# Attention, memory and two MoE layers on one core: scores of the first four tasks in fp32, two heads at once in the halves of the array, mask added by TensorE

## The chip, the cores and the metric

The program runs on one core of a Trainium2 chip. The metric is the device time of a whole execution in microseconds (us). TensorE (PE in the profile) multiplies matrices and writes PSUM, VectorE (DVE) and ScalarE (ACT) do the elementwise work, GpSimd (POOL) the maximum over partitions, and SyncE (SP) issues all DMAs.

## The reference

What is computed, cut to what matters (B=4, H=8, S=576, D=64; 2304 tokens of width 512):

```python
scores = q @ k.T / 8;  scores[causal] = -1e9
a = softmax(scores);   local = a @ v
q_p = phi(q)                            # elu(q) + 1
mem = (q_p @ M_prev) / (q_p @ z_prev + 1e-6)
x = g * mem + (1 - g) * local           # g = sigmoid(beta), per head
x = ((x @ w1) * (x @ w2)) @ w3 @ w_out  # first MoE, widths 512-1024-1024-512
h = x @ w_in                            # second MoE, widths 512-2048-512
out = (h * tanh(softplus(h))) @ w_out2
```

All arrays come as float64 weights or fp32 activations; the result is fp32.

## The kernel before

**Order of work.** The program does not run its operations in the order in which they are written. Each is recorded with an engine, a cost in ns and the buffers it reads and writes (`Recorder.op`, L82), and `schedule` (L111) then plays them through a list scheduler: PE takes its ready operations by their place in the program plus a bias, the other engines by how long a chain hangs on them. What comes out is a fixed order for each engine, and on the chip each engine works through its own order without overtaking. The costs handed to `op` therefore decide the order, and nothing else.

**Attention.** A task is a pair of heads of one batch. For batch 0 a task covers half of the queries (hf 0: queries 0 to 287 against the first 384 keys; hf 1: the rest), so tasks 0 to 3 are the hf 0 tasks of the four pairs, tasks 4 to 7 the hf 1 tasks; later tasks cover all 576 queries. Keys and queries come transposed, 64 rows a head. For a score in about fp32 precision the kernel splits them: `load_qk` (L465) loads keys and queries of one head twice, into rows 0 to 63 and again into 64 to 127 (tile `ld`, two buffers), and `prep` (L473) makes from them the tile `QK`: ACT rounds all of it to fp32r (a CAST), DVE subtracts to get what the rounding lost, in the keys' lower 64 rows and in a second copy of the queries. `SC` (L530) then gets a block of scores from two fp32r matmuls over 128 rows, high and low queries. For an hf 0 task these are three blocks of 288, 160 and 32 queries, all in one PSUM bank (tile `g`, eight banks), hence six matmuls a head. After them DVE adds the causal mask (L560, two instructions a head), ACT copies the first block to SBUF, DVE takes maxima over the blocks, POOL the maximum over partitions (L580). `SE` subtracts it (DVE) and takes the exponential (ACT; tile `e`); `AV` (L604) multiplies by V. `phi` (L488) loads the queries of both heads once more (tile `pl`) and `MEM` (L503) multiplies phi by `M`. In the first twelve tasks AV and MEM are plain fp32 matmuls, which the profile shows as two passes each.

**Weights.** The MoE weights are float64 in HBM. `conv` (L673) loads a 512 KB block and makes fp32 of it with one ACT instruction (L339) and two on DVE (L684, L686). The eight blocks of `w_out` (raw in `wA`, converted in `wB`) and the blocks of `w3` (raw in `wE` or `u`, converted in `wD`) are multiplied on the chip into one matrix (`w3_mm`, L718): 64 fp32 products of 128x512, two passes each. A group of eight products needs all eight blocks of `w_out`. Then the units of the first MoE (`g<-x,...` and `g<-u,wA`) run between the heads, and the second MoE closes the program.

Of the kernel before, what the change touches and what calls it, by code (L numbers as in the profile page):

```python
# [10 lines left out]
BF16 = mybir.dt.bfloat16  # L11
I32 = mybir.dt.int32
AF = mybir.ActivationFunctionType
ALU = mybir.AluOpType
P = 128
# [242 lines left out]
def t_mm(n, m=128):  # L258
    return max(n * 0.433 + 7, m * 0.834)
# [3 lines left out]
def kernel(  # L263
    ctx: ExitStack,
    tc: tile.TileContext,
    qk: bass.AP,
    q: bass.AP,
    v: bass.AP,
    mz: bass.AP,
    beta: bass.AP,  # L270
# [8 lines left out]
    nc = tc.nc  # L279
# [22 lines left out]
    op = rec.op  # L302
# [32 lines left out]
    def act(n, o, i, r, w, psum=False, func=AF.Copy, **kw):  # L335
        if func == AF.Copy:
            op("act", t_act(n, psum), lambda: nc.scalar.copy(out=o(), in_=i()), r, w)  # L337
        else:
            op("act", t_act(n, psum), lambda: nc.scalar.activation(out=o(), in_=i(), func=func, **kw), r, w)  # L339
# [7 lines left out]
        op(eng, t_dve(n) if eng == "dve" else t_pool(n), lambda: e.tensor_tensor(out=o(), in0=a(), in1=b(), op=alu), r, w)  # L347

    mask = const.tile([P, P], BF16, name="mask")
    eps = const.tile([P, 1], F32, name="eps")  # L350
    bt = const.tile([P, NP], F32, name="bt")
    gsc = const.tile([P, NP], F32, name="gsc")
# [11 lines left out]
    nc.vector.memset(eps[0:64], 1e-6)  # L364
    nc.vector.memset(eps[64:128], 1e-9)

    fb, fg, fm_ = Fixed(bt), Fixed(gsc), Fixed(mask)
    fx2 = [Fixed(x2d) for _ in range(2 * B)]
    Vf = buf("V", [P, 2, NJ, 2, DV])
    Vb = buf("V", [P, 2, NJ, 2, DV], F32R)  # L370
# [4 lines left out]
    def triangle():  # L375
        idx, low = tri.tile[:, 0], tri.tile[:, 1]
        nc.vector.memset(mask, 0.0)
        for y in range(1, 4):
            nc.vector.memset(mask[32 * y:32 * y + 32, 0:32 * y], NEG)
        nc.vector.memset(idx[:, 0:1], 0.0)  # L380
        for y in range(5):
            nc.vector.tensor_scalar(out=idx[:, 1 << y:2 << y], in0=idx[:, 0:1 << y], scalar1=float(1 << y), scalar2=None, op0=ALU.add)
        nc.vector.transpose(low, idx)
        nc.vector.tensor_tensor(out=low, in0=idx, in1=low, op=ALU.is_lt)
        for y in range(4):
            r = slice(32 * y, 32 * y + 32)
            nc.vector.tensor_scalar(out=mask[r, r], in0=low[r], scalar1=NEG, scalar2=None, op0=ALU.mult)

    op("dve", 1300, triangle, w=[tri, fm_])


    X = {}
# [32 lines left out]
    class Task:  # L425


        def __init__(self, g, hfs):
            self.g, self.hfs = g, hfs
            self.b, self.p = divmod(g, NP)  # L430
            self.w = HS * len(hfs)
            self.x0 = HS * hfs[0]
            self.nj = NJ if 1 in hfs else 3
            self.banks, self.masks, self.works, self.outs = LAYOUT[hfs]

        def qs(self, q0, q1):
# [25 lines left out]

    def load_qk(T, t):  # L465
        h = 2 * T.p + t
        T.qk = getattr(T, "qk", {})
        d = T.qk[t] = buf("ld", [P, KQ])
        q0 = SK + T.x0
        for y, (a, b) in enumerate({(0,): [(K3, SK + HS)], (1,): [(0, SK), (SK + HS, KQ)], (0, 1): [(0, KQ)]}[T.hfs]):  # L470
            dma(lambda a=a, b=b: d.tile[:, a:b], lambda a=a, b=b: qk[T.b, h, :, a:b], 512 * (b - a), w=[(d, y)])

    def prep(T, t):  # L473
        d = T.qk[t]
        T.Q = getattr(T, "Q", {})
        Q = T.Q[t] = buf("QK", [P, KQ + S], F32R)
        lower = HALF[1]
        parts = {(0,): [(K3, SK + HS)], (1,): [(0, SK), (SK + HS, KQ)], (0, 1): [(0, KQ)]}[T.hfs]
        for y, (a, b) in enumerate(parts):
            act(b - a, lambda a=a, b=b: Q.tile[:, a:b], lambda a=a, b=b: d.tile[:, a:b], [(d, y)], [(Q, ("k", y)), (Q, ("q", y))])  # L480
        k0 = parts[0][0]
        q0, q1 = max(parts[-1][0], SK), parts[-1][1]
        y = len(parts) - 1
        lo(SK - k0, lambda: Q.tile[lower, k0:SK], lambda: d.tile[lower, k0:SK], lambda: Q.tile[lower, k0:SK], [(d, 0), (Q, ("k", 0))], [(Q, ("k", 0))])
        lo(q1 - q0, lambda: Q.tile[:, q0 + S:q1 + S], lambda: d.tile[:, q0:q1], lambda: Q.tile[:, q0:q1], [(d, y), (Q, ("q", y))], [(Q, "l")])
        T.qkeys = [("k", 0), ("q", y), "l"]

    def phi(T):  # L488
        w = T.w
        x1 = buf("pl", [P, S])  # L490
        PH = T.PH = buf("PH", [P, S]) if T.f32 else buf("PH", [P, 2, S], F32R)
        e = PH if T.f32 else buf("t", [P, w])
        xv = lambda: x1.tile[:, 0:w]
        ev = lambda: e.tile[:, 0:w]
        dma(xv, lambda: q[T.b, 2 * T.p:2 * T.p + 2, :, T.x0:T.x0 + w].rearrange("t d s -> (t d) s"), 512 * w, w=[x1])
        act(w, ev, xv, [x1], [e], False, AF.Exp)
        act(w, xv, xv, [x1], [x1], False, AF.Identity, bias=one)
        op("dve", t_dve(w), lambda: nc.vector.scalar_tensor_tensor(out=ev(), in0=ev(), scalar=1.0, in1=xv(), op0=ALU.min, op1=ALU.max), r=[e, x1], w=[e])
        if not T.f32:
            act(w, lambda: PH.tile[:, 0, 0:w], ev, [e], [(PH, 0)])  # L500
            lo(w, lambda: PH.tile[:, 1, 0:w], ev, lambda: PH.tile[:, 0, 0:w], [e, (PH, 0)], [(PH, 1)])
# [26 lines left out]
            act(HS, lambda qs=qs, nz=nz: R.tile[0:nz, qs], lambda pn=pn, nz=nz: pn.tile[0:nz, 0:HS], [pn], [(R, (2, hf))], True)  # L528

    def SC(T, t):  # L530
        Q = T.Q[t]
        T.m = m = buf("t", [P, T.w])
        T.s = []
        mkey = []
        for i, pieces in enumerate(T.banks):
            s = gbuf()
            T.s.append(s)

            def f(s=s, pieces=pieces):
                for j, q0, q1, c in pieces:  # L540
                    o = s.tile[:, c:c + q1 - q0]
                    kc = (j * P + K3) % SK
                    for y in range(2):
                        qc = SK + y * S + q0
                        mm(o, Q.tile[:, kc:kc + P], Q.tile[:, qc:qc + q1 - q0], y == 0, y == 1)

            op("pe", sum(2 * t_mm(q1 - q0) for _, q0, q1, _ in pieces), f, r=[(Q, x) for x in T.qkeys], w=[s])
            for i2, cs, m0, m1 in T.masks:
                if i2 != i:
                    continue  # L550

                def mk(s=s, cs=cs, n=m1 - m0, m0=m0, m1=m1):
                    if len(cs) == 1:
                        o, mv = s.tile[:, cs[0]:cs[0] + n], mask[:, m0:m1]
                    else:
                        d = cs[1] - cs[0]
                        e, x = (d, 1) if 2 * d <= 512 else (d // 2, 2)
                        o = s.tile[:, 0:e * (x + 1)].rearrange("p (a c) -> p a c", c=e)[:, 0:x + 1:x, 0:n]
                        mv = mask[:, m0:m1].unsqueeze(1).to_broadcast([P, 2, n])
                    nc.vector.tensor_tensor(out=o, in0=o, in1=mv, op=ALU.add)  # L560

                op("dve", t_dve((m1 - m0) * len(cs)), mk, r=[s, fm_], w=[s])
            for j, q0, q1, c in pieces:
# [12 lines left out]
            if i + 1 == len(T.banks) or T.banks[i + 1][0][1] != pieces[0][1]:
                x = len(mkey) - 1
                a, b = mkey[x]
                mv = lambda a=a, b=b: m.tile[:, T.qs(a, b)]
                op("pool", 430 + 2.6 * (b - a), lambda mv=mv: nc.gpsimd.partition_all_reduce(mv(), mv(), P, bass_isa.ReduceOp.max), r=[(m, x)], w=[(m, x)])  # L580
# [412 lines left out]
    rec.flush()  # L993


_INS = ['qk', 'q', 'v', 'mz', 'beta', 'moe_w1', 'moe_w2', 'moe_w3', 'moe_w_out', 'moe2_w_in', 'moe2_w_out']
_OUTS = [((2304, 512), 'float32')]


# [47 lines left out]
```

## Time and profile before

| what | value |
|---|---|
| time, median of 3 runs | 965.72 us (965.35 to 968.41) |
| the profiled execution's own time | 965.84 us |
| its span | 964.1 us |
| PE busy / weight loads busy | 945.7 us (98%) / 808.9 us (84%) |
| DVE busy | 725.8 us (75%) |
| ACT busy | 607.0 us (63%) |
| POOL busy | 86.4 us (9%) |
| DMA | 96.62 MB, mean 100 GB/s |

The span runs from the first instruction to the last; 1.7 us of the execution's time lie outside it. Matmuls are pipelined: their recorded ends overlap the next starts, so the spacing of starts tells what one costs, and the busy share of PE says little by itself. PEld is the weight load that precedes each pass.

### The profile page before, as it was taken

Reading aid. Unit: us, or ns where it says so; the run is one execution under the profiler, and the core shown is the slowest. Engines: PE = TensorE matmul, PEld = TensorE weight load, DVE = VectorE, ACT = ScalarE, POOL = GpSimd, SP = SyncE. Lnnn points to the kernel's source line nnn. Section 1 sums busy time; section 2 is a strip of 40 time slices with the busy share of each in tenths; the row PEclk is TensorE's granted clock in tenths of the full one; section 3 lists DMA queues with packets and bytes.
Section 4 is the critical chain, followed back from the end, with each engine's and each line's share of the span. In section 5 each row is a group of like instructions: output and inputs, shape, how many; then the busy total and the mean of one; then the engine's idle time right before and its main releaser. Section 6 shows DMA issues by size and latency. Waiting matters only on the chain.

```text
span 964.1 us, 15222 instructions
## 1 busy us (share of the span) xinstructions
PE 945.7 (98%) x5440; PEld 808.9 (84%) x5440; DVE 725.8 (75%) x1643; ACT 607.0 (63%) x1240; POOL 86.4 (9%) x70
## 2 busy tenths in 40 slices
PE   6999999999999999999999999999999999999998
PEld 3454878778999999999999988888888888998997
DVE  7999999899999989896653987547554756565663
ACT  6677877778797778775433776446444544554653
POOL 1210012322222012120000000000000000000000
PEclk9999999999999999999999999999999999999999
DMA  9689655542433422302641740020002001100000
GB/s 351 215 246 303 201 167 153 156 141 82 142 98 91 151 75 83 107 26 83 203 153 49 228 167 1 1 81 7 1 1 83 1 0 32 46 1 17 34 1 33
DMA packets 48316, 96.62 MB, mean 100 GB/s; under 512 B 11024, under 2 KB 23344, under 8 KB 48240
## 3 DMA queue, kind: packets, MB, share of 16 engines
q1 hardware_dynamic: 48240, 95.64, 31.3%
q8 instruction: 43, 0.70, 0.3%
q14 instruction: 33, 0.27, 0.1%
HBM read 85.85 MB, written 9.77 MB: 99 GB/s over the span
## 4 chain that ended last, share of the span: by engine, by line
PE 67%; DVE 18%; ACT 6%; DMA 4%; issue 3%; SPq 1%; POOL 0%; DVEq 0%; ACTq 0%; POOLq 0%
PE g L330 67%; DVE t L347 4%; DVE QK L333 3%; DMA Rr<-d 2%; DVE e L333 1%; DVE e L347 1%; ACT t L339 1%; DVE mnl L347 1%; DVE g L560 1%; SPq L327 1%; DVE u L333 1%; DVE t L686 1%; ACT mnl L337 1%; DMA wA<-in_moe_w_out_dram 1%; ACT R L337 1%
## 5 line engine op out<-in xcount | busy, mean ns | idle before, releaser
L330 PE MATMUL g<-u,wA 128*128 128x288 f32 (+2 forms) x1008 | 162.6, 314 | 1.0 <-ACT u L337 0.6
L330 PEld LDWEIGHTS g<-u,wA 128*128 128x128 f32 x1008 | 147.2, 188 | 9.9 <-ACT u L337 1.0
L347 DVE TENSOR_TENSOR t<-g,t 128x288 f32<-128x288 f32 (+6 forms) x344 | 121.3, 380 | 22.2 <-PE g L330 14.4
L580 POOL PARTITION_ALL_REDUCE t<-t x64 | 85.8, 1342 | 352.0 <-DVE t L347 282.5
L330 PE MATMUL g<-x,wB 128*128 128x288 f32 x768 | 110.7, 298 | 0.8 <-DVE t L347 0.8
L330 PEld LDWEIGHTS g<-x,wB 128*128 128x128 f32 x768 | 104.7, 188 | 3.3 <-DVE t L347 1.4
L339 ACT ACTIVATE x<-x,two 128x512 f32<-128x512 f32 (+1 forms) x80 | 54.4, 680 | 70.8 <-DVE x L830 70.8
L339 ACT ACTIVATE x<-g 128x512 f32<-128x512 f32 (+1 forms) x98 | 55.0, 561 | 65.2 <-PE g L330 63.9
L330 PE MATMUL g<-e,V 128*65 128x320 f32 (+12 forms) x576 | 90.3, 303 | 1.9 <-ACT e L339 1.5
L833 DVE SCALAR_TENSOR_TENSOR x<-g,x 128x512 f32<-128x512 f32 (+1 forms) x80 | 51.0, 637 | 43.0 <-ACT x L339 42.6
L330 PEld LDWEIGHTS g<-e,V 128*65 128x65 f32 (+1 forms) x576 | 66.2, 136 | 20.3 <-ACT e L339 3.0
L829 DVE TENSOR_SCALAR x<-x 128x512 f32<-128x512 f32 (+1 forms) x80 | 31.8, 397 | 61.8 <-ACT x L339 60.0
L330 PE MATMUL g<-QK 128*128 128x320 f32 (+7 forms) x464 | 72.8, 298 | 5.2 <-DVE QK L333 5.1
L337 ACT CAST x<-x 128x512 fp32r<-128x512 f32 (+1 forms) x80 | 46.1, 577 | 50.4 <-DVE x L347 50.3
L330 PEld LDWEIGHTS g<-QK 128*128 128x128 f32 x464 | 64.0, 193 | 14.8 <-DVE QK L333 7.8
L333 DVE TENSOR_TENSOR t<-x 128x512 fp32r<-128x512 f32 (+1 forms) x80 | 50.9, 637 | 31.9 <-ACT x L337 30.6
L330 PE MATMUL g<-wB,wD 128*128 128x512 f32 x128 | 61.6, 619 | 3.9 <-DVE wD L686 2.1
L333 DVE TENSOR_TENSOR QK<-ld,QK 64x640 fp32r<-64x640 f32 (+1 forms) x80 | 61.7, 772 | 3.5 <-ACT QK L337 1.9
L330 PE MATMUL g<-x,wD 128*128 128x288 f32 x384 | 57.0, 298 | 0.0
L337 ACT COPY t<-g 128x288 f32<-128x288 f32 (+2 forms) x96 | 36.5, 394 | 32.5 <-PE g L330 24.7
L330 PE MATMUL g<-x,wE 128*128 128x288 f32 x384 | 56.2, 300 | 0.5 <-DVE e L347 0.4
L347 DVE TENSOR_TENSOR x<-x 128x512 f32<-128x512 f32 (+1 forms) x80 | 51.0, 637 | 6.0
(147 smaller groups left out, 1815.6 us busy)
## 6 DMA issues: line engine op xcount, KB each, us to landing
ld<-in_qk_dram SPq DMA_DIRECT2D x24, 608.0 KB
u<-in_moe_w_dram SPq DMA_DIRECT2D x26, 512.0 KB
Rr<-d SPq DMA_DIRECT2D x24, 288.0 KB
mnl<-in_moe_w_out_dram SPq DMA_DIRECT2D x11, 512.0 KB
mnl<-in_moe_w_in_dram SPq DMA_DIRECT2D x11, 512.0 KB
x2d<-t SPq DMA_DIRECT2D x16, 288.0 KB
out_dram<-x SPq DMA_DIRECT2D x18, 256.0 KB
wA<-in_moe_w_out_dram SPq DMA_DIRECT2D x8, 512.0 KB
```

The costliest lines, as they stand in the source:

```text
L327: op("sp", max(500, nbytes / 340.0), lambda: nc.sync.dma_start(out=dst(), in_=src()), r, w)
L330: nc.tensor.matmul(out=o, lhsT=lhsT, rhs=rhs, start=start, stop=stop)
L333: eng.tensor_tensor(out=o, in0=a, in1=b, op=ALU.subtract)
L337: op("act", t_act(n, psum), lambda: nc.scalar.copy(out=o(), in_=i()), r, w)
L339: op("act", t_act(n, psum), lambda: nc.scalar.activation(out=o(), in_=i(), func=func, **kw), r, w)
L347: op(eng, t_dve(n) if eng == "dve" else t_pool(n), lambda: e.tensor_tensor(out=o(), in0=a(), in1=b(), op=alu), r, w)
L560: nc.vector.tensor_tensor(out=o, in0=o, in1=mv, op=ALU.add)
L580: op("pool", 430 + 2.6 * (b - a), lambda mv=mv: nc.gpsimd.partition_all_reduce(mv(), mv(), P, bass_isa.ReduceOp.max), r=[(m, x)], w=[(m, x)])
L686: op("dve", t_dve(512), lambda: nc.vector.scalar_tensor_tensor(out=ci(), in0=ci(), scalar=3, in1=lw(), op0=ALU.logical_shift_left, op1=ALU ...
L829: op("dve", t_dve(n, True), lambda: nc.vector.tensor_scalar(out=w_(), in0=u(), scalar1=E20, scalar2=2.0, op0=ALU.min, op1=ALU.add), r=[ub_ ...
L833: op("dve", t_dve(n), lambda: nc.vector.scalar_tensor_tensor(out=u(), in0=hv(), scalar=2.0 ** -8, in1=u(), op0=ALU.mult, op1=ALU.mult), r= ...
```

## The change

For tasks 0 to 3 (`T.raw`) the two heads of a pair are loaded together: keys of both heads (head 0 in rows 0 to 63, head 1 in rows 64 to 127) and queries likewise, each value once. `prep` does nothing for them. One operation computes both heads' scores: for each of the three blocks an fp32 matmul of head 0 in the upper 64 rows of the array into one bank and one of head 1 in the lower 64 rows into another, and then for each bank a bf16 matmul of a 128x128 unit matrix with the mask, which adds the mask in PSUM. DVE's mask instructions go for these four tasks (`CFG["PEM"]`), and `phi` reads the queries from the same tile and loads none of its own. The unit matrix is built by DVE at the start. The new operation has a cost of its own, so the scheduler's orders change too.

```diff
+    PEM=4,
...
+        nc.vector.memset(unit, 0.0)
+        for y in range(4):
+            r = slice(32 * y, 32 * y + 32)
+            nc.vector.tensor_tensor(out=unit[r, r], in0=idx[r], in1=low[r], op=ALU.is_equal)
...
+            self.raw = hfs == (0,)
...
     def load_qk(T, t):
+        if T.raw:
+            if t == 0:
+                T.kq = buf("ld", [P, KQ])
+                dma(lambda: T.kq.tile[:, K3:SK], lambda: kp[T.b, h:h + 2, :, K3:SK].rearrange("t d s -> (t d) s"), 512 * (SK - K3), w=[(T.kq, 0)])
+                dma(lambda: T.kq.tile[:, SK:SK + T.w], lambda: q[T.b, h:h + 2, :, T.x0:T.x0 + T.w].rearrange("t d s -> (t d) s"), 512 * T.w, w=[(T.kq, 1)])
+            return
...
     def prep(T, t):
+        if T.raw:
+            return
...
+        xi, xr = xv, x1
+        if T.raw:
+            xi, xr = lambda: T.kq.tile[:, SK:SK + w], (T.kq, 1)
+        else:
+            dma(xv, ...)
...
+            low = {c: (m0, m1) for i2, cs, m0, m1 in T.masks for c in cs if i2 == i and T.i < CFG["PEM"]}
+            def fr(ss, pieces=pieces, low=low):
+                for j, q0, q1, c in pieces:
+                    kc, qc = (j * P + K3) % SK, SK + q0 - T.x0
+                    for s, r in zip(ss, HALF):
+                        mm(s.tile[:, c:c + q1 - q0], T.kq.tile[r, kc:kc + P], T.kq.tile[r, qc:qc + q1 - q0], True, c not in low)
+                    for s in ss:
+                        if c in low:
+                            m0, m1 = low[c]
+                            mm(s.tile[:, c:c + m1 - m0], unit, mask[:, m0:m1], False, True)
...
+            if T.raw:
+                if t == 0:
+                    T.pair = [gbuf(), gbuf()]
+                    op("pe", sum(2 * max(0.84 * (q1 - q0), 107) + 75 for _, q0, q1, _ in pieces), lambda fr=fr, ss=T.pair: fr(ss),
+                       r=[(T.kq, 0), (T.kq, 1), fm_, fu], w=T.pair)
+                s = T.pair[t]
...
             for i2, cs, m0, m1 in T.masks:
-                if i2 != i:
+                if i2 != i or T.i < CFG["PEM"]:
                     continue
```

How the orders move, at three places. First PE at the start of the program, where `g<-QK` are a head's scores, `g<-wB,wD` the products of the weights and `g<-e_...,V` a head's product with V. Before, from the second head's scores on:

```order
L330 MATMUL g<-QK 128x288 x2
L330 MATMUL g<-QK 128x160 x2
L330 MATMUL g<-QK 128x32 x2
L330 MATMUL g<-wB,wD 128x512 x4
L330 MATMUL g<-e_177,V 65x288
L330 MATMUL g<-e_177,V 65x160
L330 MATMUL g<-e_177,V 65x32
```

Now, from the first pair's last mask on (`g<-mask,unit`; `g<-ld` are raw scores, x2 being the two heads):

```order
L332 MATMUL g<-mask,unit 128x32
L332 MATMUL g<-PH,M 128x288
L332 MATMUL g<-PH,M 2x288
L332 MATMUL g<-wB,wD 128x512
L332 MATMUL g<-e_168,V 65x288
L332 MATMUL g<-e_168,V 65x160
L332 MATMUL g<-e_168,V 65x32
L332 MATMUL g<-ld 128x288 x2
```

One product of the weights instead of four stands ahead of the first head's product with V, and the second pair's scores come before the rest.

Second DVE at the start, after the mask is built: `QK` is the splitting, `t<-g,t` the maxima, `wA`, `wB` the conversion of a block of `w_out`. Before:

```order
L333 TENSOR_TENSOR QK<-ld,QK 64x384
L333 TENSOR_TENSOR QK<-ld,QK 128x288
L498 SCALAR_TENSOR_TENSOR PH<-PH,pl 128x288
L560 TENSOR_TENSOR g<-g,mask 128x2x128
L333 TENSOR_TENSOR QK<-ld,QK 64x384
L560 TENSOR_TENSOR g<-g,mask 128x32
L333 TENSOR_TENSOR QK<-ld,QK 128x288
L684 TENSOR_SCALAR wA<-wA 128x512
L686 SCALAR_TENSOR_TENSOR wB<-wB,wA 128x512
L347 TENSOR_TENSOR t<-g,t 128x160
```

Now:

```order
L520 SCALAR_TENSOR_TENSOR PH<-PH,pl 128x288
L349 TENSOR_TENSOR t<-g,t 128x160
L730 TENSOR_SCALAR wA<-wA 128x512
L349 TENSOR_TENSOR t<-g,t 128x32
L349 TENSOR_TENSOR t<-g,t 128x160
L732 SCALAR_TENSOR_TENSOR wB<-wB,wA 128x512
L349 TENSOR_TENSOR t<-g,t 128x32
L730 TENSOR_SCALAR wE<-wE 128x512
```

The splitting and the masks are gone, and the maxima of both heads stand side by side, the first of them ahead of the first conversion.

Third SP's queue of DMAs in the same stretch. Before:

```order
L327 DMA ld<-in_qk_dram 128x672
L327 DMA wA<-in_moe_w_out_dram 128x1024
L327 DMA wE<-in_moe_w_dram 128x1024
L327 DMA wA<-in_moe_w_out_dram 128x1024 x3
L327 DMA ld<-in_qk_dram 128x672
L327 DMA V<-in_v_dram 128x396
L327 DMA wA<-in_moe_w_out_dram 128x1024
L327 DMA u<-in_moe_w_dram 128x1024
L327 DMA wA<-in_moe_w_out_dram 128x1024 x3
```

Now:

```order
L329 DMA wA<-in_moe_w_out_dram 128x1024
L329 DMA wE<-in_moe_w_dram 128x1024
L329 DMA V<-in_v_dram 128x396
L329 DMA wA<-in_moe_w_out_dram 128x1024
L329 DMA ld<-in_kp_dram 128x384
L329 DMA ld<-in_q_dram 128x288
L329 DMA wA<-in_moe_w_out_dram 128x1024 x3
L329 DMA u<-in_moe_w_dram 128x1024
L329 DMA wA<-in_moe_w_out_dram 128x1024 x3
```

Ahead of the last block of `w_out` stand three loads of 128x672 before (the first is the program's first DMA), and two pairs of 128x384 and 128x288 now.

## Rows read from the trace of the kernel before

**Rows 1.** The page, busy time, share of the span and instructions of each engine.

```profile
PE 945.7 (98%) x5440; PEld 808.9 (84%) x5440; DVE 725.8 (75%) x1643; ACT 607.0 (63%) x1240; POOL 86.4 (9%) x70
```

**Rows 2.** Chain that ended last, whole span: start us, us, what.

```profile
421.82 538.52 PE g L330 x2863
```

**Rows 3.** Busy time in four stretches; the columns stand in the first row.

```profile
core 0: us, PE busy (x) PEld busy (x) DVE busy (x) ACT busy (x) POOL busy (x), PEclk, DMA share, GB/s
0.00:28.00 28.00, 18.26 (x52) 9.00 (x52) 22.96 (x70) 17.24 (x32) 4.74 (x9) 1.00 0.93 353
28.00:96.00 68.00, 67.57 (x228) 34.19 (x227) 63.98 (x162) 47.72 (x100) 9.50 (x7) 1.00 0.79 249
96.00:420.00 324.00, 319.82 (x2292) 291.01 (x2291) 302.41 (x789) 254.45 (x578) 67.00 (x50) 1.00 0.41 123
420.00:964.00 544.00, 540.09 (x2875) 474.68 (x2873) 336.40 (x625) 287.54 (x534) 5.19 (x4) 1.00 0.17 55
```

**Rows 4.** The same chain in the first 30 us.

```profile
26.05 0.69 DVE wB L686
...
26.77 3.28 PE g L330 x13
```

**Rows 5.** PE in order of time, 0 to 66 us: start us, us, instructions [idle before].

```profile
5.09 1.77 PE L330 MATMUL g<-QK 128*128 128x288 f32 x6 [5.09 <-DVE QK L333]
...
27.74 1.23 PE L330 MATMUL g<-PH,M 128*128 128x288 f32 x4
28.89 0.88 PE L330 MATMUL g<-QK 128*128 128x288 f32 x6
...
34.02 1.17 PE L330 MATMUL g<-QK 128*128 128x288 f32 x6
...
39.78 0.89 PE L330 MATMUL g<-QK 128*128 128x288 f32 x6
40.52 1.96 PE L330 MATMUL g<-wB,wD 128*128 128x512 f32 x4
42.32 1.01 PE L330 MATMUL g<-e,V 128*65 128x288 f32 x6
43.16 3.68 PE L330 MATMUL g<-wB,wD 128*128 128x512 f32 x8
46.44 1.28 PE L330 MATMUL g<-QK 128*128 128x288 f32 x6
```

**Rows 6.** DVE's groups by shape, 0 to 66 us: count | busy us, mean ns.

```profile
L333 DVE TENSOR_TENSOR QK<-ld,QK 64x384 fp32r<-64x384 f32 x8 | 5.3, 662 | 0.8 <-ACT QK L337 0.4
...
L333 DVE TENSOR_TENSOR QK<-ld,QK 128x288 fp32r<-128x288 f32 x9 | 4.5, 503 | 0.5 <-ACT QK L337 0.3
...
L560 DVE TENSOR_TENSOR g<-g,mask 128x256 f32<-128x256 f32 x8 | 3.4, 426 | 1.2 <-PE g L330 1.2
...
L347 DVE TENSOR_TENSOR t<-g,t 128x160 f32<-128x160 f32 x8 | 2.6, 320 | 0.7 <-ACT t L337 0.5
...
L498 DVE SCALAR_TENSOR_TENSOR PH<-PH,pl 128x288 f32<-128x288 f32 x4 | 1.8, 450 | 0.1
L560 DVE TENSOR_TENSOR g<-g,mask 128x32 f32<-128x32 f32 x8 | 1.6, 194 | 0.1
L347 DVE TENSOR_TENSOR t<-g,t 128x32 f32<-128x32 f32 x8 | 1.5, 184 | 0.1
...
L387 DVE TENSOR_SCALAR mask<-t 32x32 bf16<-32x32 f32 x4 | 0.7, 173 | 0.1
```

**Rows 7.** ACT's group of the splitting, 0 to 66 us.

```profile
L337 ACT CAST QK<-ld 128x672 fp32r<-128x672 f32 x8 | 6.0, 750 | 3.0 <-DMA ld<-in_qk_dram 3.0
```

**Rows 8.** DMA issues, 0 to 66 us: count, KB each.

```profile
ld<-in_qk_dram SPq DMA_DIRECT2D x8, 336.0 KB
...
pl<-in_q_dram SPq DMA_DIRECT2D x5, 144.0 KB
```

**Rows 9.** Weight loads by group, 0 to 96 us.

```profile
L330 PEld LDWEIGHTS g<-QK 128*128 128x128 f32 x68 | 10.4, 213 | 10.2 <-DVE QK L333 7.8 <-issue 1.1 <-DVE wE L684 0.5
```

More of the change, by code (lines that the diff above doesn't have):

```diff
@@ L267 @@
     q: bass.AP,
+    kp: bass.AP,
     v: bass.AP,
@@ L349 @@
     mask = const.tile([P, P], BF16, name="mask")
+    unit = const.tile([P, P], BF16, name="unit")
     eps = const.tile([P, 1], F32, name="eps")
@@ L365 @@
     nc.vector.memset(eps[64:128], 1e-9)
-    fb, fg, fm_ = Fixed(bt), Fixed(gsc), Fixed(mask)
+    fb, fg, fm_, fu = Fixed(bt), Fixed(gsc), Fixed(mask), Fixed(unit)
     fx2 = [Fixed(x2d) for _ in range(2 * B)]
@@ L387, in triangle @@
             nc.vector.tensor_scalar(out=mask[r, r], in0=low[r], scalar1=NEG, scalar2=None, op0=ALU.mult)
-    op("dve", 1300, triangle, w=[tri, fm_])
+    op("dve", 1300, triangle, w=[tri, fm_, fu])
     X = {}
@@ L494, in phi @@
         ev = lambda: e.tile[:, 0:w]
-        dma(xv, lambda: q[T.b, 2 * T.p:2 * T.p + 2, :, T.x0:T.x0 + w].rearrange("t d s -> (t d) s"), 512 * w, w=[x1])
-        act(w, ev, xv, [x1], [e], False, AF.Exp)
-        act(w, xv, xv, [x1], [x1], False, AF.Identity, bias=one)
+        xi, xr = xv, x1
+        if T.raw:
+            xi, xr = lambda: T.kq.tile[:, SK:SK + w], (T.kq, 1)
+        else:
+            dma(xv, lambda: q[T.b, 2 * T.p:2 * T.p + 2, :, T.x0:T.x0 + w].rearrange("t d s -> (t d) s"), 512 * w, w=[x1])
+        act(w, ev, xi, [xr], [e], False, AF.Exp)
+        act(w, xv, xi, [xr], [x1], False, AF.Identity, bias=one)
         op("dve", t_dve(w), lambda: nc.vector.scalar_tensor_tensor(out=ev(), in0=ev(), scalar=1.0, in1=xv(), op0=ALU.min, op1=ALU.max), r=[e, x1], w=[e])
@@ L530, in SC @@
     def SC(T, t):
-        Q = T.Q[t]
         T.m = m = buf("t", [P, T.w])
@@ L535, in SC, with f @@
         for i, pieces in enumerate(T.banks):
-            s = gbuf()
-            T.s.append(s)
-            def f(s=s, pieces=pieces):
+            low = {c: (m0, m1) for i2, cs, m0, m1 in T.masks for c in cs if i2 == i and T.i < CFG["PEM"]}
[8 more added lines that the diff above has]
+                            mm(s.tile[:, c:c + m1 - m0], unit, mask[:, m0:m1], False, True)
+            def f(s=None, pieces=pieces, low=low):
+                Q = T.Q[t]
                 for j, q0, q1, c in pieces:
@@ L544, in f @@
                         qc = SK + y * S + q0
-                        mm(o, Q.tile[:, kc:kc + P], Q.tile[:, qc:qc + q1 - q0], y == 0, y == 1)
-            op("pe", sum(2 * t_mm(q1 - q0) for _, q0, q1, _ in pieces), f, r=[(Q, x) for x in T.qkeys], w=[s])
+                        mm(o, Q.tile[:, kc:kc + P], Q.tile[:, qc:qc + q1 - q0], y == 0, y == 1 and c not in low)
+                    if c in low:
+                        m0, m1 = low[c]
+                        mm(s.tile[:, c:c + m1 - m0], unit, mask[:, m0:m1], False, True)
+            if T.raw:
[4 more added lines that the diff above has]
+                s = T.pair[t]
+            else:
+                s = gbuf()
+                op("pe", 75 * len(low) + sum(2 * t_mm(q1 - q0) for _, q0, q1, _ in pieces), lambda f=f, s=s: f(s),
+                   r=[(T.Q[t], x) for x in T.qkeys] + [fm_, fu] * (len(low) > 0), w=[s])
+            T.s.append(s)
             for i2, cs, m0, m1 in T.masks:
-                if i2 != i:
+                if i2 != i or T.i < CFG["PEM"]:
                     continue
@@ L993 @@
     rec.flush()
-_INS = ['qk', 'q', 'v', 'mz', 'beta', 'moe_w1', 'moe_w2', 'moe_w3', 'moe_w_out', 'moe2_w_in', 'moe2_w_out']
+_INS = ['qk', 'q', 'kp', 'v', 'mz', 'beta', 'moe_w1', 'moe_w2', 'moe_w3', 'moe_w_out', 'moe2_w_in', 'moe2_w_out']
 _OUTS = [((2304, 512), 'float32')]
@@ L1014 @@
     k = _np.pad(inputs["k"].transpose(0, 1, 3, 2), ((0, 0), (0, 0), (0, 0), (0, nj * P_ - s)))
-    k = _np.concatenate([k[..., 3 * P_:], k[..., :3 * P_], lay["q"]], axis=-1)
+    lay["kp"] = _np.concatenate([k[..., 3 * P_:], k[..., :3 * P_]], axis=-1)
+    k = _np.concatenate([lay["kp"], lay["q"]], axis=-1)
     lay["qk"] = _np.concatenate([k, k], axis=2)
```

## The prediction

> **What bounds the kernel now.** I read the chain of waits first: its last piece is PE alone, 538.52 us of matmuls from 421.82 us to the end [rows 2]. Then the stretches [rows 3]: of the span's first 28 us PE is busy for 18.26, after that almost always: 67.57 of 68, 319.82 of 324, 540.09 of 544 us. The change touches nothing behind the first 66 us, so the end moves by two things: the PE work added or taken away, and the time in which PE has nothing to do. That idle time is 28 - 18.26 = 9.7 us at the start, 0.4 us up to 96 us and 4.2 us up to 420 us. PE is 98% busy on the page [rows 1], but a busy PE at the start is not a full one: the first head's six score matmuls take 1.77 us, later heads' 0.88 to 0.89 [rows 5], so of the start more than 9.7 us is loose.
>
> What the start waits for is read in the chain: DVE converts the eighth block of w_out until 26.74 us, and the eighth product of the weights starts at 26.77 [rows 4]; from there PE has a backlog. In these 28 us DVE is busy for 22.96 and the DMA engines for 93% [rows 3]. Both are candidates, and the change relieves both.
>
> **The change, part by part.** The sum is made against the profiled execution's 965.84 us (span 964.1 and 1.7 outside); the median is 965.72.
>
> DVE loses per head the keys' difference 0.662, the queries' 0.503, and two mask additions 0.426 + 0.194: 1.785 us, for eight heads 14.3 us [rows 6]. It gains the unit matrix, four compares like the mask's 0.173 and a memset: under 0.9 us. ACT loses eight casts of 0.750, 6.0 us [rows 7]. DMA loses, per pair, two loads of 336 KB and one of 144 KB and gains as much as one of 336 KB: 480 KB, four times [rows 8]. None of this is on the path by itself; each acts through PE's waits, in five terms.
>
> *Term 1, the start.* How much earlier is the eighth product? At best by what DVE no longer does ahead of that conversion. Before, three heads' splitting and masks stand ahead of it, 3 x 1.785 = 5.4 us. The new order puts one more head's maxima (0.320 + 0.184) and one more phi (0.450) ahead of it: net 4.4 us. By DMA the gain is smaller: ahead of the last block stand three loads of 336 KB and one of 144 KB before and two of 336 KB now, 480 KB or 1.4 us at 353 GB/s [rows 3, 8]. At worst it is nothing: each engine keeps its order, and the new one puts the maxima of both heads ahead of the first conversion. They wait for the pair's scores and ACT's copy, and later maxima of the second pair wait for scores that PE reaches only behind the first head's product with V. POOL's two maxima of a pair now follow each other as well. Queued behind a late maximum on DVE are the conversions, and PE waits for these. I take the middle of 0 and 4.4, 2.2, which holds the DMA's gain and some of DVE's.
>
> *Term 2, work done ahead.* At its eighth product the old PE has done three heads' scores and one memory product; the new order has four heads and two memory products there. That work falls away later: 40.52 - 39.78 = 0.74 for a head, 28.89 - 27.74 = 1.15 for the memory product [rows 5]: 1.9 us.
>
> *Term 3, stalls of the splitting.* Two heads in the full stretch take 1.17 and 1.28 instead of 0.89 us [rows 5]: their second matmul waits for the low queries, which DVE makes last. Raw scores wait for a load alone: 0.28 + 0.39 = 0.7 us saved. Late next would be the load; it is asked for when an `ld` buffer is free, which is now after both heads' scores and phi, and behind it on SP wait the weights' loads. I cost that at nothing, as each of the two buffers now holds a whole pair, so that a load has a pair's time to land.
>
> *Term 4, the raw scores themselves.* A pair costs 2 x 0.74 = 1.48 us now. The trace has fp32 passes over the same 288, 160 and 32 columns: a head's product with V, 43.16 - 42.32 = 0.84 us for two passes of each [rows 5]. With the halves side by side a pair takes 0.84, one after the other 1.68. A mask matmul isn't in the trace. Its bounds are nothing (hidden) and a whole small matmul with its weight load in the open, 0.74 / 6 = 0.12 and 0.213 [rows 5, 9]. With six masks a pair is between 0.84 and 1.68 + 2.0 = 3.7 us, a change of -0.6 to +2.2. I take 1.26 (one half's second pass beside the other's first) and 0.12 for each mask: 2.0, +0.5. The first two pairs fall into the start, where PE waits anyway; two count: +1.0, ends -1.3 and +4.4.
>
> *Term 5, relief behind 28 us.* DVE is busy for 63.98 of 68 and then 302.41 of 324 us, and PE idles for 4.2 us up to 420 [rows 3]. PE comes about 5 us earlier to this stretch, DVE has some 13 us less to do before it. I take 1.0 of the 4.2 us; ends 0 and 2.5. From 260 us on the order is nearly the old one, so nothing is moved there.
>
> At nothing: the unit matrix (DVE then waits for the first queries' exponential; if not, 0.9 us on the first pair), the key array without copies (made outside the device time), two banks of PSUM taken at once (eight exist).
>
> Sum: -2.2 - 1.9 - 0.7 + 1.0 - 1.0 = -4.8; 965.84 - 4.8 = 961.0 us.
>
> **Rivals.** *The start gains nothing.* DVE's gain is lost in the order, as told in term 1. For it: PE has 9.7 us idle there because several engines wait for each other in turn, and the new order has fewer products ahead of the first head's product with V. Against it: both loaded resources have less to do. Terms 1 and half of 5 go: 961.0 + 2.2 + 0.5 = 963.7.
>
> *The array pays for each change between halves and whole.* Six changes a pair, each of which leaves one weight load of 0.213 in the open [rows 9]: +1.3 a pair, +2.6 for two: 963.6. For it: the masks alternate with the scores block by block. Against it: little, since the trace has no matmul in half the rows; the matmuls that it has follow each other without such gaps, and by them the sum stays at 961.0. The Trainium skill speaks for it in "TensorEngine Tiling (Array Packing)", Key Properties: changing the tiling mode, and not just the tile, drains TensorE; no run here shows that yet, and by that rule the time is this rival's 963.6.
>
> *Slower.* The halves don't overlap at all, and every weight load of the pair is in the open: 1.68 + 12 x 0.213 + 6 x (0.12 + 0.213) = 6.2, +4.8 a pair. Two pairs in the full stretch cost 9.5, and the first two eat term 1: 965.84 - 1.9 - 0.7 + 9.5 - 1.0 = 971.7. Without term 1 the kernel is slower from a pair of 1.48 + 3.6 / 2 = 3.3 us on, and by 0.3% from 4.7 us. Against it: today's fp32 passes, with a weight load each, cost 0.84 a head, only 0.10 more than six fp32r matmuls [rows 5], so their loads are not in the open.
>
> *Much faster.* DVE's full 4.4 in term 1, no cost in term 4, 2.5 in term 5: 965.84 - 4.4 - 1.9 - 0.7 - 2.5 = 956.3.
>
> **How the numbers follow.** The forecast has 0.57, the idle start 0.14, the changes of mode 0.12, slower 0.09, much faster 0.08. The forecast's own range is 958 to 964; the range for 8 in 10 is 956.5 to 966. A measurement of this kernel tells about 0.3%, 2.9 us, from no change. Faster than 962.8: the much faster case and all but 0.08 of the forecast, 0.57. Within: that 0.08 and the first two rivals, 0.34. Slower: 0.09.
>
> **What would show it.** Term 1: the eighth product of the weights at about 24.6 us instead of 26.8. Term 2: four heads' scores and two memory products before it. Terms 3 and 4: a pair of raw scores with its masks takes about 2 us in the full stretch; 3.3 or more speaks for the slower case, and gaps between mask and next block of 0.2 for the changes of mode. Term 5: less than 4.2 us of idle PE from 96 to 420 us. It is wrong if PE's backlog starts no earlier than 26.8 us, or if PE idles more than 0.4 us in the stretch after it.

## The result: slower by 0.7%, and the profile after

The changed kernel takes 973.57 us (median of 6 runs, 970.14 to 974.93) against 965.74 for the kernel before beside it (6 runs). The ratio is 1.0073 [1.0054, 1.0092]; 961.0 was forecast. The profiled execution has a span of 971.1 us against 964.1.

The page's busy time by engine, after:

```profile
PE 949.6 (98%) x5464; PEld 808.7 (83%) x5464; DVE 715.1 (74%) x1616; ACT 601.7 (62%) x1232; POOL 86.2 (9%) x70
```

Against [rows 1] DVE has 10.7 us less to do and ACT 5.3: what the change takes from them is gone. PE is 3.9 us busier; four raw pairs with their masks, at 0.5 us more than before each, make 2.1 of it, so some of its work ran slower. The last piece of the chain of waits (start, length):

```profile
428.93 538.63 PE g L332 x2863
```

It is as long as in [rows 2] and starts 7.1 us later. The whole loss of this execution therefore lies ahead of 429 us, and the second half of the program plays no part. The stretches of [rows 3], with one cut out of the start:

```profile
0.00:28.00 28.00, 19.13 (x64) 8.98 (x65) 18.83 (x64) 14.12 (x28) 6.00 (x10) 0.94 0.84 319
24.00:28.00 4.00, 3.19 (x4) 1.40 (x5) 3.69 (x9) 1.75 (x3) 0.00 (x0) 0.57 0.36 144
28.00:96.00 68.00, 68.00 (x233) 32.93 (x231) 56.34 (x141) 45.32 (x94) 7.86 (x6) 1.00 0.75 238
96.00:420.00 324.00, 316.64 (x2253) 286.57 (x2253) 296.30 (x769) 249.16 (x567) 65.31 (x49) 1.00 0.42 122
```

Two things stand out. In the start the granted clock is 0.94 instead of 1.00, and 0.57 in its last 4 us, close to the lower of TensorE's two levels (1.2 and 2.4 GHz). And from 96 to 420 us PE idles for 324 - 316.64 = 7.4 us, against 4.2 before, although DVE is less busy there (296.30 against 302.41). PE in order of time, in the start (start us, us, instructions [idle before, and what ended it]):

```profile
3.71 1.33 PE L332 MATMUL g<-ld 64*128 64x288 f32 x4 [3.71 <-DMA ld<-in_q_dram]
...
7.11 2.35 PE L332 MATMUL g<-PH,M 128*128 128x288 f32 x4
11.99 2.07 PE L332 MATMUL g<-wB,wD 128*128 128x512 f32 x2 [2.53 <-DVE wD L732]
13.85 1.86 PE L332 MATMUL g<-e,V 128*65 128x288 f32 x6
15.64 1.33 PE L332 MATMUL g<-ld 64*128 64x288 f32 x4
...
20.20 1.96 PE L332 MATMUL g<-wB,wD 128*128 128x512 f32 x4
24.81 4.26 PE L332 MATMUL g<-wB,wD 128*128 128x512 f32 x6 [2.64 <-DVE wD L732]
28.90 1.23 PE L332 MATMUL g<-PH,M 128*128 128x288 f32 x4
30.05 1.13 PE L332 MATMUL g<-wB,wD 128*128 128x512 f32 x2
...
34.61 0.76 PE L332 MATMUL g<-ld 64*128 64x288 f32 x4
35.30 0.28 PE L332 MATMUL g<-mask,unit 128*128 128x128 bf16 x2
35.52 0.54 PE L332 MATMUL g<-ld 64*128 64x160 f32 x4
35.99 0.29 PE L332 MATMUL g<-mask,unit 128*128 128x128 bf16 x2
36.20 0.41 PE L332 MATMUL g<-ld 64*128 64x32 f32 x4
36.55 0.21 PE L332 MATMUL g<-mask,unit 128*128 128x32 bf16 x2
36.61 1.04 PE L332 MATMUL g<-e,V 128*65 128x288 f32 x6
```

The pair at 34.61 ends at 36.61: 2.00 us, as forecast. Ahead of it PE works at half pace twice. The first spell reaches from its first matmul into the pair at 15.64: the head's product with V at 13.85 takes 1.86 us, the one at 36.61 1.04; the granted clock in the rows doesn't show this spell, the durations do. (The kernel before starts slowly too, but its first product with V, at 17.81 us, takes 1.01 us and so stands behind that spell.) The second is behind the idle 2.64 us: six passes of the weights take 4.09 us from 24.81 to 28.90, where the mended start shown below has 3.06 for the same six. The eighth product of the weights (two passes), which the chain before showed at 26.77 [rows 4], starts at 30.05: 3.3 us later; one memory product (`g<-PH,M`, 1.15 us) now stands ahead of it that came after it before.

What DVE and ACT waited for in that time (DVE's two rows, then ACT's):

```profile
15.82 0.79 DVE L349 TENSOR_TENSOR e<-g,t 128x288 f32<-128x288 f32 x3 [2.56 <-PE g L332]
...
21.94 1.28 DVE L732 SCALAR_TENSOR_TENSOR wB<-wB,wA 128x512 int32<-128x512 int32 x1 [0.82 <-ACT wB L341]
```

```profile
15.75 0.39 ACT L339 COPY R<-g 1x288 f32<-1x288 f32 x1 [2.45 <-PE g L332]
...
24.95 0.60 ACT L341 ACTIVATE e<-e 128x480 f32<-128x480 f32 x1 [1.94 <-DVE e L349]
```

DVE and ACT stand still for PE's slow product with V, with the weights' conversions behind them in their queues, and PE then stands still for these conversions. The three wait for each other in a ring, so DVE's lighter load does not come through. Behind the start, what PE waited for from 96 to 430 us (total us, times, longest):

```profile
PE g L332 <- DVE t L349: 3.4, 3, 1.8
PE g L332 <- ACT mnl L339: 2.4, 4, 0.7
PE g L332 <- ACT u L339: 1.1, 1, 1.1
PE g L332 <- ACT e L341: 1.0, 1, 1.0
```

Before, the longest such wait was 0.8 us, in this line:

```profile
PE g L330 <- DVE t L347: 1.7, 2, 0.8
```

The changed kernel's waits are on softmax and output steps that the change does not touch.

### The profile page after: what moved, and what is told of

The parts are those of the page before. It is cut to its first block, busy times and chain, and to the rows that moved or that the text cites. A ratio compares the mean times of both kernels' runs of the same rounds, so it can differ in the third digit from the quotient of the medians.

```text
span 971.1 us, 15231 instructions
## 1 busy us (share of the span) xinstructions
PE 949.6 (98%) x5464; PEld 808.7 (83%) x5464; DVE 715.1 (74%) x1616; ACT 601.7 (62%) x1232; POOL 86.2 (9%) x70
## 4 chain that ended last, share of the span: by engine, by line
PE 71%; DVE 16%; ACT 5%; DMA 3%; issue 3%; POOL 0%; SPq 0%; DVEq 0%; ACTq 0%
PE g L332 71%; DVE t L349 4%; DVE QK L335 2%; DVE e L349 2%; DVE mnl L349 1%; ACT t L341 1%; DMA Rr<-d 1%; DVE g L606 1%; DVE e L335 1%; DVE u L335 1%; DMA u<-in_moe_w_dram 1%; ACT QK L339 1%; ACT R L339 1%; DVE cp L699 1%; DMA cp<-d 1%
## 5 line engine op out<-in xcount | busy, mean ns | idle before, releaser
L349 DVE TENSOR_TENSOR t<-g,t 128x320 f32<-128x320 f32 (+7 forms) x344 | 121.8, 382 | 21.8 <-PE g L332 13.2
L332 PE MATMUL g<-QK 128*128 128x64 f32 (+3 forms) x416 | 62.3, 292 | 1.1 <-ACT mnl L339 1.1
L332 PEld LDWEIGHTS g<-QK 128*128 128x128 f32 x416 | 56.2, 190 | 4.3 <-ACT mnl L339 1.4
L332 PEld LDWEIGHTS g<-x,wE 128*128 128x128 f32 x384 | 52.3, 188 | 4.6 <-DVE t L349 2.1
```

## Experiments

Three numbers tell the kernels below apart. S is the start of the eighth product of the weights. L is the time from there to the first matmul of the second stage; from that one to the end of the span it is 389.2 us in the two kernels above and in the one told 1000 ns with a mended start. PE's idle time in L is L less the time that PE is busy in it. For the two kernels above, in the columns of [rows 3]:

```profile
26.77:574.84 548.07, 543.22 (x3638) 476.59 (x3638) 470.94 (x1170) 390.45 (x865) 81.70 (x61) 1.00 0.47 144
30.05:581.90 551.85, 542.80 (x3640) 474.81 (x3640) 462.54 (x1144) 387.39 (x858) 80.20 (x60) 1.00 0.46 141
```

L is 3.8 us longer, PE's idle time in it 4.2 us, and its busy time 0.4 us shorter. In all kernels but r1_cost (551.8) PE is busy for 542.4 to 546.6 us of L, so L moves mostly by PE's waits; the 4 us between them also hold spells at the lower clock. S, L and the idle time are of one profiled execution each, the time is a median. One kernel's executions differ (965.04 to 970.26 us in 29 runs of the kernel before), so 2 or 3 us of L in one trace prove nothing by themselves.

| kernel | S | L | PE idle in L | time, ratio to before |
|---|---|---|---|---|
| before | 26.77 | 548.06 | 4.85 | 965.74 to 967.22, measured anew for each group |
| changed | 30.05 | 551.85 | 9.05 | 973.57, 1.0073 [1.0054, 1.0092] |
| k1_pinned | 28.74 | 550.97 | 6.61 | 970.65, 1.0034 [1.0022, 1.0045] |
| c1_order | 26.97 | 551.00 | 5.87 | 968.48, 1.0011 [0.9999, 1.0024] |
| p2_raw_only | 26.68 | 553.09 | 10.65 | 969.65, 1.0028 [1.0011, 1.0045] |
| p1_mask_only | 28.73 | 550.42 | 5.63 | 971.85, 1.0047 [1.0030, 1.0064] |
| r1_cost | 27.92 | 572.04 | 20.23 | 989.15, 1.0223 [1.0197, 1.0249] |
| e1_ebuf | 29.83 | 554.26 | 9.96 | 975.18, 1.0089 [1.0069, 1.0109] |
| w_before | 26.59 | 549.84 | 6.08 | 966.66, 0.9995 [0.9985, 1.0006] |
| w_after | 25.51 | 553.68 | 9.01 | 970.54, 1.0037 [1.0020, 1.0054] |
| w_k1 | 26.66 | 552.35 | 9.17 | 971.02, 1.0039 [1.0026, 1.0052] |
| wc_900 | 27.90 | 553.30 | 10.30 | 971.27, 1.0041 [1.0025, 1.0056] |
| wc_1000 | 25.69 | 549.63 | 7.03 | 966.96, 0.9995 [0.9982, 1.0008] |
| wc_1050 | 25.51 | 558.76 | 12.14 | 974.70, 1.0077 [1.0062, 1.0092] |
| wc_1100 | 25.75 | 550.05 | 5.72 | 966.86, 0.9995 [0.9982, 1.0008] |
| wc_1383 | 26.72 | 556.40 | 12.17 | 974.26, 1.0071 [1.0056, 1.0086] |
| c_1000 | 28.45 | 552.14 | 6.71 | 970.07, 1.0025 [1.0010, 1.0040] |
| c_1100 | 28.14 | 549.25 | 4.46 | 968.49, 1.0018 [1.0007, 1.0028] |

**The work in the old order (k1_pinned).** The scheduler is given the old operations with their old costs; those that the change removes emit nothing, and the raw pair stands where the first head's scores stood.

```diff
+            if T.raw:
+                op("act", t_act(b - a), lambda: None, [(d, y)], [(Q, ("k", y)), (Q, ("q", y))])
+                continue
...
+                op("pe", sum(2 * t_mm(q1 - q0) for _, q0, q1, _ in pieces), fr, r=[(T.Q[t], x) for x in T.qkeys], w=[s])
```

> All four raw pairs with their masks on TensorE, but every engine works in the order of the kernel before: the scheduler is still given the old operations with their old costs, and those that fall away (splitting on ScalarE and VectorE, masks on VectorE) issue nothing; the queries for phi are loaded as before. Theory A (the loss comes from the new order, not from the new work): no slower than before, 959 to 965 us, and the start's eighth product comes no later than 27 us. Theory B (the new work itself costs the time: row halves, mode changes, masks, both heads at once): slower than before whatever the order, 968 to 974 us.

The old order does not restore the gain: theory A fails and theory B's 968 to 974 us is met. What speaks against B's reason, that the new work costs whatever the order, comes with the told costs below. S is 2.0 us late here too:

```profile
11.54 2.07 PE L332 MATMUL g<-wB,wD 128*128 128x512 f32 x2 [2.09 <-DVE wD L747]
14.19 5.49 PE L332 MATMUL g<-wB,wD 128*128 128x512 f32 x6 [0.57 <-DVE wB L747]
19.47 1.05 PE L332 MATMUL g<-e,V 128*65 128x288 f32 x6
```

The first eight passes run at half pace to 19.5 us, the six from 14.19 on in 0.88 us each. L is 2.9 us longer. PE idles 1.8 us more in it, of which one wait of 1.45 us at 90 us is for a load of V, and the granted clock falls once, to 0.83 over 10 us, behind two waits of 0.7 us:

```profile
420.00:430.00 10.00, 8.92 (x57) 8.56 (x58) 9.97 (x26) 8.14 (x21) 3.74 (x3) 0.83 0.01 2
```

**The old work in another order (c1_order).** The kernel before, with the first halves' scores told to the scheduler as 596 ns instead of 690.

```diff
-            op("pe", sum(2 * t_mm(q1 - q0) for _, q0, q1, _ in pieces), f, r=[(Q, x) for x in T.qkeys], w=[s])
+            op("pe", 596 if T.hfs == (0,) else sum(2 * t_mm(q1 - q0) for _, q0, q1, _ in pieces), f, r=[(Q, x) for x in T.qkeys], w=[s])
```

> The kernel before, every instruction kept; only the cost that the scheduler is told for a head's scores in tasks 0 to 3 is 596 ns instead of 690, so the orders change. Theory A: the time moves by 2 us or more from 965.7, either way. Theory B: 965.7 within 1.5 us.

The interval holds 1, so it settles nothing by itself; L is 2.9 us longer in its one trace, with not one instruction changed and 1.0 us more idle time. No third order of the old work was run, so how good an order the kernel before has is not known.

**Each half of the change alone (p2_raw_only, p1_mask_only).** First raw scores with the masks on VectorE (`PEM=0`), then masks on TensorE with the split scores (`self.raw = False`).

> Raw scores of both heads as in the changed kernel, but the masks stay on VectorE for all tasks (the scheduler makes an order of its own for it). Theory A: the masks are not the cause, and the time is that of one more order, 964 to 975 us, with waits at other places than the changed kernel. Theory B, if masks and mode changes are the cost: 965 us or less; if the raw scores are: 972 to 974.

> The kernel before with the masks of all heads of the first halves added by TensorE, and scores from the rounded pairs as before: the masks leave VectorE, the raw scores are left out. TensorE gets 12 more small matmuls, about 0.6 us for each pair as the trace of the changed kernel shows masks; VectorE loses the same mask additions. Theory (order): the time is set by where the new order has TensorE wait between 96 and 430 us, so it is within 2 us of 970 (PE idle there 6 to 9 us, against 4.2 before). Rival (each part has its own price, and they add): masks take the part of the loss that raw scores alone (2.7 us) left of the whole change's 7.1, so 971 to 972. Rival (raw scores are what costs): masks alone are free, 964 to 967 and PE idle of 4 to 5 us in that stretch.

Both lose, in different places: raw scores keep S and lose in L (one wait on `t` of 2.7 us at 187 us), masks alone lose 2.0 us in S and 2.4 in L. The theory met the time of masks alone but not its place: PE idles only 324 - 320.73 = 3.3 us from 96 to 420 us there. The rival met the time as well (971.85 in 971 to 972): by the ratios the halves lose 2.7 and 4.5 us, together the whole change's 7.1. By S and L of the single traces they lose 4.9 and 4.3, which is more. So these two runs don't rule out that each half has a price of its own; the runs below with unchanged instructions do, as no fixed price can move by 8 us. (p1_mask_only has 24 matmuls more than the kernel before, 5464 against 5440, not 12.)

**The changed kernel in another order (r1_cost).** Only the cost of a raw pair told to the scheduler changes, from 1192 ns to 2000.

```diff
-                    op("pe", sum(2 * max(0.84 * (q1 - q0), 107) + 75 for _, q0, q1, _ in pieces), lambda fr=fr, ss=T.pair: fr(ss),
+                    op("pe", 2000, lambda fr=fr, ss=T.pair: fr(ss),
```

> The changed kernel, every instruction kept; the scheduler is told 2000 ns for a raw pair with its masks, what the trace shows, instead of 1192 ns. Theory A: the time differs from 973.6 by 2 us or more. Theory B: 973.6 within 1.5 us. If it is the wrong cost that made the order bad, this one comes out faster, 962 to 970 us.

2000 ns is what a pair really takes, and the kernel becomes 15.6 us slower (14.5 by the ratios): a truer cost does not give a better order. Its waits from 96 to 430 us:

```profile
PE g L332 <- DVE t L349: 10.3, 12, 1.6
```

They crowd in one place; PE from 380 to 396 us, and the clock in that stretch:

```profile
383.38 1.97 PE L332 MATMUL g<-e,V 128*65 128x320 f32 x15 [1.52 <-ACT t L339]
385.19 2.11 PE L332 MATMUL g<-QK 128*128 128x256 f32 x14
388.72 0.66 PE L332 MATMUL g<-PH,M 128*128 128x288 f32 x3 [1.42 <-DVE t L349]
390.98 0.43 PE L332 MATMUL g<-PH,M 128*4 128x288 f32 x2 [1.60 <-DVE t L349]
```

```profile
390.00:400.00 10.00, 7.48 (x39) 6.09 (x40) 9.94 (x23) 8.01 (x19) 1.82 (x2) 0.66 0.20 64
```

The same instructions stand so that PE meets DVE's maxima with nothing but other attention steps between them, and behind the waits the granted clock is 0.66 on top.

**The start at full pace (w_after, w_before, w_k1).** Zero matmuls fill PE's idle time in the start, in the order given: 6 ahead of the first scores and 12 ahead of the first and of the fifth product of the weights. They add nothing to the output. The old kernel gets 8 and 8 ahead of its first scores and first product, the pinned one 6 and 12.

```diff
+                if T.i == 0:
+                    idle_mm(ss[0].tile[:, 0:512], 6, True)
...
+                if f == 0 and c in (0, 4):
+                    idle_mm(ps.tile[:, 0:512], {0: 12, 4: 12}[c], c == 0)
```

> The changed kernel in its own order, with matmuls of zeros put into TensorE's idle stretches of the start: 6 ahead of the first scores, 12 ahead of the first product of the weights and 12 ahead of the fifth (they add zeros or are overwritten). Theory C (TensorE works at half its pace in the start for longer than before and falls back to it after its second idle stretch, 0.57 granted from 24 to 28 us): passes of the products take 0.43 us from the first on, the eighth product ends 2 us or more earlier than 31.0, and the whole comes to 969 to 972 us. Theory A (waits in the middle, from the order): 973 to 974, since nothing behind the start changes.

> The kernel before with the same matmuls of zeros, 8 ahead of the first scores and 8 ahead of the first product. Theory C: its own first three products, now at 0.85 us a pass, run at 0.43; but it waits for conversions anyway, so 964 to 966.5 us. Theory A: 966 within 1.

> The raw scores in the old order, with matmuls of zeros ahead of the first scores (6) and of the first product (12). Theory C: the four products from 11.5 to 19.5 us take half as long, the eighth ends near 27 us instead of 29.7, and the whole comes to 966 to 968.5 instead of 970.65. If it stays above 970, the clock in the start is not what made the raw scores slower in the old order.

The mended start of the changed kernel:

```profile
11.21 1.13 PE L332 MATMUL g<-wB,wD 128*128 128x512 f32 x2 [0.88 <-DVE wD L740]
12.17 1.01 PE L332 MATMUL g<-e,V 128*65 128x288 f32 x6
...
18.70 2.75 PE L332 MATMUL g<-zer 128*128 128x512 bf16 x12
21.29 3.23 PE L332 MATMUL g<-wB,wD 128*128 128x512 f32 x6
24.35 1.23 PE L332 MATMUL g<-PH,M 128*128 128x288 f32 x4
25.51 1.13 PE L332 MATMUL g<-wB,wD 128*128 128x512 f32 x2
```

No pass runs at half pace any more (six from 21.29 to 24.35 in 3.06 us), the waits of 2.56 us on DVE and 2.45 us on ACT for the first product with V shrink to 0.80 and 0.69, and S falls from 30.05 to 25.51, with the order unchanged. That removes the start's loss, and shows its cause: the slow pace, fed by the ring of waits. Of the 4.5 us the time keeps 3.0 (3.5 by the ratios, with an uncertainty of 2.5 by their intervals). L is 1.8 longer in the trace, with the same 9.0 us of idle PE; one spell at a granted clock of 0.83 from 360 to 370 us accounts for it. In the old kernel the same help moves S by 0.2 us: there was no such loss to mend. In the pinned kernel S falls by 2.1 us and the time not at all (971.02 against 970.65), as PE idles 2.6 us more in L. By that run's own expectation the slow start is not what makes the pinned kernel slower than the one before.

**A second buffer for `e` (e1_ebuf).** DVE's wait at 15.82 us is for the only buffer of the first heads' exponentials; here second heads have their own.

```diff
+            if T.raw and t == 1:
+                tag = "e1"
...
```

> The changed kernel, but the exponentials of a raw pair's second head get a buffer of their own (that of a later task), so that VectorE need not wait for the first head's product with V before it subtracts for the second. Theory D (this wait of 2.56 us on VectorE holds the conversions behind it and with them the start): no such wait, the eighth product ends 2 us earlier, 970 to 972 us. Theory A: another order, so any time from 965 to 980. The order of the whole program changes with it, so only the start is compared by parts.

S gains 0.2 us, L loses 2.4. The wait for the buffer is gone, but DVE now waits 2.28 us for ACT's conversion (at 17.13 us) in its place. The buffer alone does not keep the start late; but the order changed as well, so the test is not clean.

**The told cost with the mended start (wc_900, wc_1000, wc_1050, wc_1100, wc_1383).** w_after with the same line as in r1_cost, set to these numbers.

> The changed kernel with zero matmuls in its start, and the raw pair's cost told to the scheduler as 1000 ns where it was 1191: the same instructions in another order. Theory (order): the eighth product of the weights starts within 1 us of 25.5 us, as with the other told cost, but PE's idle time between 96 and 430 us differs by 1.5 us or more from that kernel's, and the time with it, anywhere from 964 to 980. Rival (the work itself costs, the order does not): 970.5 within 1.2 us.

> As the kernel with 1000 ns, the raw pair's cost told as 1100 ns. Theory (order): the time follows PE's idle time between 96 and 430 us one for one, and differs from the kernels told 1000, 1191 and 1383 by 1.5 us or more from at least one. Rival (the work itself costs): 970.5 within 1.2 us.

> As the kernel with 1000 ns, the raw pair's cost told as 1383 ns, twice what the scheduler counts for one head's split scores before. Theory (order): again another sum of waits between 96 and 430 us, 964 to 980; the best of the orders shows what the change is worth when its order is as good as the one before, by the terms of the forecast 961 to 965 with the start kept at full pace. Rival (the work itself costs): 970.5 within 1.2 us, as all of these.

> The changed kernel with zero matmuls in its start and 900 ns told: another order of the same instructions. Theory (time over full pace behind the eighth product is set by the order, the work is not): TensorE's work between the eighth product and the second stage is 535 to 537 us as in the others, the rest of the time follows its waits; best case for an order with as few waits as before (13.1 us) is 965.5 to 967. Rival (a better order lets the change win): under 964.

> As wc_900 with 1050 ns told, between the two told costs that gave 966.9. Theory: an order lying between two good ones need not be good, since nearly every row moves; 966 to 975, following the waits. Rival (smooth in the told cost): 966.9 within 0.8 us.

The 535 to 537 and 13.1 us in the expectation of wc_900 come from a sum over the distances between matmuls' starts that no view shows; the table has PE's idle time instead. From 966.86 to 974.70 us with the same instructions: the rival in which the work sets the time falls, and so does a smooth dependence, since 1050 lies between the two best and is as slow as the slowest. The time follows PE's idle time in L: 5.72 and 7.03 us in the two good orders, 9.01 in w_after, 10.30 in wc_900, 12.14 and 12.17 in the two slow ones. S lies between 25.51 and 27.90, so not every one of these orders has a fully mended start. The two good orders reach the kernel before and don't pass it. wc_1000 in the stretches of [rows 3]:

```profile
28.00:96.00 68.00, 66.39 (x226) 31.98 (x224) 57.42 (x144) 45.73 (x95) 7.85 (x6) 1.00 0.78 242
96.00:420.00 324.00, 318.80 (x2286) 289.44 (x2285) 300.15 (x781) 253.22 (x574) 66.73 (x50) 1.00 0.41 121
```

PE idles 1.6 and 5.2 us there, 2.2 more than before, with S 1.1 us earlier.

**The good orders without the mended start (c_1000, c_1100).** The changed kernel with the told cost alone.

> The changed kernel without zero matmuls, the raw pair's cost told as 1000 ns: the start as the change leaves it, the order that gave 966.96 with the start mended. Theory (start and order add): the eighth product of the weights starts at 29 to 31 us, and the time is 3 to 4.5 us above the mended kernel's, 970 to 971.5. Rival (later waits take the start's loss up): within 1.2 us of 967. Rival (the order alone is the cause, and the mended start gained by its new order in name only): the same 967 with the eighth product still at 30.

> As c_1000 with 1100 ns told, the order that gave 966.86 with the start mended. Theory (start and order add): 970 to 971.5, the eighth product at 29 to 31 us. Rivals: within 1.2 us of 967.

S is at 28.45 and 28.14, earlier than expected, and 2.8 and 2.4 us later than with zero matmuls. Against the kernel before, run beside them, the ratios rise from 0.9995 to 1.0025 and 1.0018: 2.9 and 2.2 us, with an uncertainty of 1.9 and 1.6 us by their intervals. That is what the start costs, in orders that lose little behind it. Start and order are two causes; in w_after and wc_1000 the gain of a mended start stays, with PE's idle time in L unchanged within 0.4 us. In wc_1100 later waits take up 1.3 us of it, in the pinned kernel all, so that the two add is not a rule. In microseconds c_1100 falls short of its expectation, as its start loses less than in the changed kernel.

## Why the prediction was wrong, point by point

The forecast was 4.8 us less, the profiled execution took 7.0 more: 11.9 apart. S was to be 24.6 and was 30.05, 5.5 of it. L was to fall to 548.06 - 1.9 - 0.7 + 1.0 - 1.0 = 545.5 and was 551.85, the other 6.4. Of these, 5.2 are PE's idle time (9.05 us where 4.85 - 1.0 was forecast), and 1.2 are in PE's busy time, which was to fall by 1.6 and fell by 0.4.

*Term 1, the start (-2.2), failed.* "Each engine keeps its order" was seen as a reason to gain nothing; that it could lose was left out, the term's ends being 0 and 4.4. What took its place is in the runs: longer idle waits for conversions, after which PE runs at half pace, and through the ring DVE and ACT wait in turn. The zero matmuls give back all of the loss and 1.3 us more (S 25.51). The forecast 24.6 was reached in no kernel; in w_after DVE still waits 0.59 and 0.64 us for ACT's conversions.

*Term 2, work ahead (1.9), held as to the order:* at S four heads' scores and two memory products are done, one of each more than before. What it was worth is within L and not separable.

*Term 3 (0.7):* raw scores showed no stall between their matmuls, as said; the gain is within L and not separable.

*Term 4 (a pair 2.0 us) held in its sum:* 2.00. Its parts differ: scores 0.69 + 0.47 + 0.35 = 1.51 where 1.26 was taken, masks 0.22 + 0.21 + 0.06 = 0.49 where 0.72 was, by the starts of the rows from 34.61 on. The scores lie nearer to two halves one after the other (1.68) than to full overlap (0.84); that the sum met 2.0 is in part luck, two errors that cancel. The slower case's mechanism, a pair of 6.2 us, is wrong; that its 971.7 us lies near the measured time is luck, the time was lost elsewhere.

*Term 5, relief behind 28 us (-1.0), failed,* with its ends 0 and 2.5. PE idles 7.4 us from 96 to 420 us instead of 4.2. It is the sentence "From 260 us on the order is nearly the old one, so nothing is moved there" that is wrong: waits of 0.64 and 1.19 us stand ahead of 264 and 278 us, of 1.14 ahead of 368 and of 0.73 twice at 423 and 424. From 260 to 430 us, before and after:

```profile
260.00:430.00 170.00, 168.63 (x1301) 163.96 (x1300) 155.99 (x395) 132.98 (x306) 32.13 (x24) 1.00 0.32 93
260.00:430.00 170.00, 164.76 (x1260) 158.41 (x1259) 151.43 (x385) 127.84 (x296) 32.05 (x25) 1.00 0.31 90
```

PE idles 1.4 us there before and 5.2 after. In the two traces PE's order is the same only from about 325 us on and DVE's from about 365. The order behind the start is made anew from told costs, and the changed kernel's instructions, without zero matmuls, ran between 968.49 (c_1100) and 989.15 us (r1_cost). The range of the forecast held nothing for it.

*The rivals.* "The start gains nothing" named the right place but stopped at zero. The array's price for changes of mode, 1.3 us a pair on top of the 2.0, did not show: whatever it is, the 2.00 us hold it, and it decided nothing. The first sign by which the prediction called itself wrong was met, S after 26.8; the second was not, since PE is busy for 68.00 of 68 us in the stretch after it.

Left open: which step of an order brings its waits behind the start; and why the old order with the lighter work idles 1.8 us more in L. One wait for V is seen; for the rest no run isolates it.

## What to carry to other kernels

Taking work from an engine can gain nothing where that engine, another and PE wait for each other in turn, and can lose when the new order leaves PE idle long enough to slow down (2.5 and 2.6 us here). Where a scheduler makes the order from told costs, compare a change over several told costs before judging the work: here five other told costs moved the time by up to 8 us, as much as the whole change. Price the disorder of a new order in the range, on both sides, also far behind the edit.

## What the runs showed of the hardware

Two fp32 matmuls with 64 rows each overlapped in part: the three blocks of a pair, both heads, took 1.51 us in halves, where one head's product with V over the same columns in the whole array took 0.84 [rows 5]; a mask matmul between them took 0.03 to 0.11. Around PE's wait of 2.64 us in the changed kernel's start the granted clock was 0.57 over 4 us; after waits of 1.4 to 1.6 us in r1_cost it was 0.66 over 10 us, and a single wait of 2.15 us in w_after's middle left 0.83 over 10 us. But the wait of 1.8 us ahead of 195 us in the changed kernel left 1.00 (190 to 200 us), and two of 0.7 us in k1_pinned were followed by 0.83: the length of one wait does not tell. So a wait can cost more than its length; with zero matmuls in its place no pass in the start ran at half pace.
